# Halo slots of x: transposing transfers in place of GpSimd copies, with a newly searched order

## The chip, the cores and the metric

The kernel runs on one core of a Trainium2 chip. The metric is device time in microseconds, the median of several runs; lower is better. A core has five engines that run at the same time, each through its own list of instructions in order: PE (TensorE, matrix products), DVE (VectorE), ACT (ScalarE), POOL (GpSimd) and SP (which here only issues transfers). DMA engines move data between the chip's main memory and SBUF, the on-chip memory of 128 partitions. PSUM (here called ps) receives what PE computes and is read by DVE and ACT.

## The reference

The input x has 2 sequences of 16000 rows (time steps) of 512 values. The steps are: a depthwise convolution over time with 3 taps, silu, four rounds of residual vector quantization (pick the nearest of 8 code vectors, subtract it), and a second depthwise convolution over the sum of the picked vectors.

```python
xp = jnp.pad(x, ((0,0),(pad,pad),(0,0)))          # pad = 1
for i in range(K):                                # K = 3
    z = z + xp[:, i:i+T, :] * dw_enc[i][None, None, :]
z = _silu(z)
res = z
for s in range(Nq):                               # Nq = 4, C = 8 codes each
    cb = codebooks[s]
    d2 = |res|^2 - 2 res.cb + |cb|^2
    sel = cb[d2.argmin(-1)]
    q = q + sel
    res = res - sel
for i in range(K):
    y = y + qp[:, i:i+T, :] * dw_dec[i][None, None, :]
```

For this study the first loop matters: row t of z needs rows t-1, t and t+1 of x.

## The kernel before

**Tiles.** Each sequence is cut into 9 tiles of G x 128 rows, with G = 6, 8 and seven times 16 in the first sequence and the reverse in the second: 18 tiles, numbered 0 to 17. Neighbouring tiles overlap by four rows, and the outermost rows of a tile at such a joint are not stored, because they lack a true neighbour. Variable `st` describes a tile: `row0` is its first row, G its number of slots.

**Layout of x.** `XT` (two buffers, NX = 2, used by even and odd tiles) holds a tile transposed: the 512 channels lie in 4 groups over 128 partitions; along the free dimension lie G + 2 slots of 128 rows. Row p*G + g of the tile is column p of slot g + 1. So the row before is the same column one slot lower, and the row after one slot higher. The three taps thus read `X[:, i, k:k + G, :]` for k = 0, 1, 2 (line 523). Slots 0 and G + 1 are the halo: slot 0 must hold slot G shifted by one column, and slot G + 1 must hold slot 1 shifted by one column the other way.

**Loading** (`load`, lines 490 to 503). SP issues G transposing transfers for slots 1 to G (line 496). Then POOL fills the halo: the copy at line 502 writes slot 0 from slot G, the copy at line 503 writes slot G + 1 from slot 1. The one column in each halo slot that no row of the tile fills is set to zero (memsets recorded as line 354). A tap reads all G + 2 slots, so it waits for all transfers and both copies; a buffer's next load waits for the taps of two tiles before.

**After the load.** `front` (line 507) runs the taps: six products by a weight for each half of the channels (lines 524 on ACT, 525 on DVE), two additions into ZB (line 367, the line of every DVE tensor_tensor), then exp on ACT (530) and 1 + exp on DVE or ACT. `front2` takes the reciprocal on ACT (542) and multiplies (the gate, 367). `select` (575) scores the first three codebooks on PE (560) and decides on DVE; `windows` (656) transposes the picks into OHW; `resid` (674) subtracts the picked vectors: PE writes the product into ps, and either DVE adds it to ZB (702), or PE adds ZB too (693) and ACT copies the sum back (700); `back` (734) computes the output on PE (751 to 755), ACT moves it from ps to YB (759), and POOL issues the stores (782).

**The order.** No engine's list is written by hand. Every step is handed to a planner (`Plan`, line 17) with an engine, an estimated duration, a key (kind of step, tile, position), and what it reads and writes. `Plan.order` places the steps one by one: the step that could start first, and among equals the one of lowest rank. A rank is made of the tables in `WHEN` (line 248): for each kind of step and for the head, the middle and the tail of the run, an offset in tiles and a slope. `SHARE` says how much DVE's queue must be shorter than ACT's for an eviction of ps to go to DVE; `SLACK` says how much later than DVE ACT may finish an either/or step and still take it; `QUOTA` limits how many pieces of ps may be held for each of the two. The steps are then emitted in that order. The planner also puts filler matmuls (line 802) into PE's gaps. So the durations that the planner is told decide only the order and who does what; what the chip takes is another matter.

Of the kernel before, what the change touches and what calls it, by code (L numbers as in the profile page):

```python
# [12 lines left out]
ACT = mybir.ActivationFunctionType  # L13
# [3 lines left out]
class Plan:  # L17
# [16 lines left out]
    def add(self, engine, cost, key, fn, reads=(), writes=(), take=None, free=None, hold=None, tail=0.0, after=(), dest=None, box=None, mm=0):  # L34
        n = len(self.steps)
        deps = set(after)
        for t in reads:
            if t in self.writer:
                deps.add(self.writer[t])
            self.readers.setdefault(t, []).append(n)  # L40
        for t in writes:
            if t in self.writer:
                deps.add(self.writer[t])
            deps.update(self.readers.get(t, ()))
            self.writer[t] = n
            self.readers[t] = []
        deps.discard(n)
        self.steps.append({"n": n, "e": engine, "c": cost, "k": key, "fn": fn, "deps": sorted(deps), "take": take, "free": free,
                           "hold": hold, "tail": tail, "dest": dest, "box": box, "mm": mm})
        return n  # L50
# [163 lines left out]
def kernel(  # L214
# [8 lines left out]
    nc = tc.nc  # L223
    P = nc.NUM_PARTITIONS
    B, T, D = x.shape
# [16 lines left out]
    PAIR = 1  # L242
    NX, NE, NZ, NOH, NY = 2, 3, 4, 4, 4
    NA = 4
    SHARE = (11.59, 1.54, -2.01)
    SLACK = (0.29, 0.1, -0.82)
    QUOTA = {"ACT": 3, "DVE": 4}
    WHEN = {"setup": ((-0.301, 1.023), (0.403, 0.68), (0.166, 0.636)), "load": ((-2.074, 0.878), (-2.063, 0.738), (-2.063, 0.878)),
            "pad": ((-1.367, 0.11), (-1.736, 0.139), (-2.291, 0.134)), "taps": ((-0.056, 0.643), (-0.338, 0.654), (0.494, 1.172)),
            "exp": ((0.772, 0.385), (0.713, 0.297), (0.924, 0.12)), "plus1": ((1.188, 0.422), (0.353, 0.234), (0.286, 0.554)),  # L250
            "recip": ((0.485, 0.701), (0.412, 0.023), (1.293, 0.525)), "gate": ((-0.006, 0.61), (0.929, 0.495), (1.31, 0.636)),
            "score0": ((-0.15, 0), (1.321, 0.2), (0.126, 0.312)), "decide": ((1.768, 0.427), (0.519, 0.211), (0.108, 0.835)),
            "win0": ((2.318, 0), (2.302, 0), (3.131, 0.025)), "resid": ((1.585, 0.808), (1.683, 0.698), (1.872, 0.836)),
            "score3": ((2.128, 0.792), (2.59, 0.231), (3.148, 1.482)), "decide3": ((1.628, 0.493), (2.782, 0.723), (3.385, 0.635)),
            "win3": ((3.135, 0.158), (3.009, 1.183), (3.633, 0.195)), "back": ((2.837, 0.37), (3.155, 1.136), (4.214, 0.566))}
    assert B == len(SIZES) and T >= GM * P and GM <= 16

    xf = x.flatten_outer_dims()
# [7 lines left out]
    tiles = []  # L266
    for b, sizes in enumerate(SIZES):
        done = 0
        for g in sizes:
            r = g * P  # L270
            t0 = max(0, min(done - 2, T - r))
# [9 lines left out]
    def sb(shape, dt, name):  # L281
        return const.tile(list(shape), dt, name=name)
# [14 lines left out]
    XT = [sb([P, KT, GM + 2, P], BF16, f"XT{b}") for b in range(NX)]  # L297
# [26 lines left out]

    plan = Plan(NA, (3, len(tiles) - 3), SHARE, SLACK, QUOTA, WHEN)
    add = plan.add
# [26 lines left out]
    def pool_memset(t, v, tok, cost, key):  # L353
        add("POOL", cost, key, lambda: nc.gpsimd.memset(t, v), writes=tok)
# [4 lines left out]

    def dve_memset(t, v, tok, cost, key):  # L360
        add("DVE", cost, key, lambda: nc.vector.memset(t, v), writes=tok)

    for b in range(NX):
        pool_memset(XT[b][:, :, 0, 0:2], 0.0, [("XE", b)], 0.3, ("setup", -29, 0))

    def tt(out, a, b, op, cost, key, reads, writes, **kw):
        add("DVE", cost, key, lambda: nc.vector.tensor_tensor(out=out, in0=a, in1=b, op=op), reads, writes, **kw)  # L367
# [122 lines left out]
    def load(st):  # L490
        n, G = st["n"], st["G"]
        X = XT[n % NX]
        src = xf[st["row0"]:st["row0"] + G * P, :].rearrange("(p g) d -> g p d", g=G)

        def one(g):
            nc.sync.dma_start_transpose(out=X[:, :, g + 1, :], in_=src[g])  # L496
        for g in range(G):
            add("SP", 1.56, ("load", n, 0.01 * g), lambda g=g: one(g), [], [("X", n % NX, g + 1)], tail=1.5)
        key = ("pad", n - 20 * (n == 0), 0)
        if n < NX or tiles[n - NX]["G"] != G:  # L500
            pool_memset(X[:, :, G + 1, P - 2:P], 0.0, [("X", n % NX, G + 1)], 0.3, key)
        add("POOL", 1.0, key, lambda: nc.gpsimd.tensor_copy(X[:, :, 0, 1:P], X[:, :, G, 0:P - 1]), [("X", n % NX, G)], [("XE", n % NX)])  # L502
        add("POOL", 1.0, key, lambda: nc.gpsimd.tensor_copy(X[:, :, G + 1, 0:P - 1], X[:, :, 1, 1:P]), [("X", n % NX, 1)], [("X", n % NX, G + 1)])  # L503

    state = {}

# [257 lines left out]
    def store(st, Y, g0, g1):  # L764
# [16 lines left out]
        for p0, p1, lo, hi in split:  # L781
            nc.gpsimd.dma_start(out=view[p0:p1, lo:hi, :], in_=Y[p0:p1, lo - g0:hi - g0, :])  # L782

    load(tiles[0])
    setup()
    for group in GROUPS:
        halves = {}
        for st in group:
            if st["n"]:
                load(st)  # L790
            for h in range(2):
                halves[st["n"], h] = front(st, h)
        for st in group:
            for h in range(2):
                front2(st, h, *halves[st["n"], h])
        for st in group:
            select(st)
            resid(st)
            back(st)
# [40 lines left out]
```

## Time and profile before

| | |
|---|---|
| median of 7 runs | 732.02 us (729.85 to 736.03) |
| profiled run, whole | 733.12 us |
| its span, first to last instruction | 731.3 us |
| mean granted TensorE clock | 0.955 |
| halo copies on POOL, lines 502 and 503 | 18 and 18; busy 23.4 and 33.0 us |
| transposing transfers on SP, line 496 | 252; 1.27 us each in the median to issue, 3.9 us to landing |
| evictions of resid on ACT (700) and on DVE (702) | 287 and 145; busy 246.8 and 150.6 us |
| taps on DVE (525) and on ACT (524) | 205 and 11 |

"Span" is the time between the first and the last instruction; "busy" is the time in which an engine ran at least one instruction. A group is named by its line, its engine and what it writes and reads (`ZB<-ZB,ps` writes ZB and reads ZB and ps). In lists of waits, `A <- B` means that A started when B was done, and the figures are the total in us, the number of times and the longest.

### The profile page before, as it was taken

Reading aid. Unit: us, or ns where it says so; the run is one execution under the profiler, and the core shown is the slowest. Engines: PE = TensorE matmul, PEld = TensorE weight load, DVE = VectorE, ACT = ScalarE, POOL = GpSimd, SP = SyncE. Lnnn points to the kernel's source line nnn. Section 1 sums busy time; section 2 is a strip of 40 time slices with the busy share of each in tenths; the row PEclk is TensorE's granted clock in tenths of the full one; section 3 lists DMA queues with packets and bytes.
Section 4 is the critical chain, followed back from the end, with each engine's and each line's share of the span. In section 5 each row is a group of like instructions: output and inputs, shape, how many; then the busy total and the mean of one; then the engine's idle time right before and its main releaser. Section 6 shows DMA issues by size and latency. Waiting matters only on the chain.

```text
span 731.3 us, 24280 instructions
## 1 busy us (share of the span) xinstructions
PE 577.0 (79%) x10605; PEld 285.4 (39%) x10681; DVE 680.9 (93%) x1251; ACT 666.8 (91%) x590; POOL 133.3 (18%) x199
## 2 busy tenths in 40 slices
PE   5887676796788879798676878778876889899994
PEld 2343232344334434443243343434343444444442
DVE  8989999898999999999999999999999999999892
ACT  6888989889999999999999999999999899998755
POOL 2101022000120331212123302103113110201114
PEclk9999797899989989999999999999999999999998
DMA  5455524625153462818258441716453210303215
GB/s 111 94 95 100 118 53 123 109 46 80 58 125 52 83 122 56 161 54 161 65 125 166 105 73 36 129 46 151 102 90 132 81 38 2 119 5 114 89 45 195
DMA packets 148049, 67.81 MB, mean 93 GB/s; under 512 B 139776, under 2 KB 139808, under 8 KB 147944
## 3 DMA queue, kind: packets, MB, share of 16 engines
q1 hardware_dynamic: 137088, 33.06, 26.6%
q0 software_dynamic: 10640, 32.78, 14.3%
q8 instruction: 83, 1.36, 0.8%
q10 hardware_dynamic: 216, 0.43, 0.2%
q14 instruction: 22, 0.18, 0.1%
HBM read 0.43 MB, written 32.77 MB: 45 GB/s over the span
## 4 chain that ended last, share of the span: by engine, by line
DVE 53%; PE 25%; ACT 10%; issue 7%; DMA 3%; SPq 1%; POOL 0%; DVEq 0%; POOLq 0%; ACTq 0%
DVE ZB L702 12%; PE ps L694 8%; DVE ZB L367 7%; DVE TB L525 7%; PE ps L693 6%; DVE TA L367 6%; PE ps L560 4%; ACT ZB L700 4%; DVE TA L525 3%; ACT YB L759 3%; DVE EX L532 2%; PE ps L802 2%; DMA XT<-in_x_dram 2%; DVE OHW L671 2%; SPq L496 1%
## 5 line engine op out<-in xcount | busy, mean ns | idle before, releaser
L694 PE MATMUL ps<-OHW,CBN 128*128 128x512 bf16 (+1 forms) x768 | 269.3, 388 | 20.1 <-DVE ZB L702 12.8
L700 ACT CAST ZB<-ps 128x1024 bf16<-128x1024 f32 (+2 forms) x287 | 246.8, 953 | 27.4 <-PE ps L694 24.5
L693 PE MATMUL ps<-ZB,IDENT 128*128 128x512 bf16 (+1 forms) x517 | 201.5, 390 | 19.8 <-DVE ZB L702 11.7
L702 DVE TENSOR_TENSOR ZB<-ZB,ps 128x1024 bf16<-128x1024 bf16 (+2 forms) x145 | 150.6, 1054 | 2.2 <-PE ps L694 1.4
L782 POOL DMA_DIRECT2D out_dram<-YB x130 | 74.3, 575 | 352.2 <-ACT YB L759 348.9
L759 ACT CAST YB<-ps 128x1024 bf16<-128x1024 f32 x126 | 123.6, 1041 | 5.1 <-PE ps L751 2.4
L694 PEld LDWEIGHTS <-CBN 128*128 128x128 bf16 x768 | 74.9, 99 | 134.1 <-issue 63.7
L530 ACT ACTIVATE EX<-ZB 128x4096 bf16<-128x4096 bf16 (+2 forms) x36 | 115.5, 3209 | 5.3 <-DVE ZB L367 5.2
L542 ACT ACTIVATE EX<-EX 128x4096 bf16<-128x4096 bf16 (+2 forms) x36 | 114.6, 3194 | 0.2
L560 PEld LDWEIGHTS <-ZB 128*32 128x32 bf16 x8064 | 75.2, 95 | 58.9 <-issue 55.4
L560 PE MATMUL ps<-ZB 128*32 128x64 bf16 x8064 | 88.0, 197 | 12.2 <-issue 5.9
L525 DVE TENSOR_SCALAR TB<-XT,WENC 128x2048 bf16<-128x2048 bf16 (+2 forms) x137 | 92.6, 688 | 0.2
L802 PE MATMUL ps<-MSK,IDENT 128*128 128x512 bf16 x242 | 68.9, 424 | 20.1 <-issue 5.8
L751 PE MATMUL ps<-WDEC,OHW 128*128 128x512 bf16 x219 | 68.0, 381 | 15.2 <-ACT YB L759 3.8
L693 PEld LDWEIGHTS <-IDENT 128*128 128x128 bf16 x517 | 51.7, 100 | 64.8 <-issue 14.6
L367 DVE TENSOR_TENSOR ZB<-ZB,EX 128x4096 bf16<-128x4096 bf16 (+2 forms) x36 | 74.0, 2055 | 1.3 <-ACT EX L542 1.1
L367 DVE TENSOR_TENSOR ZB<-TA,TB 128x4096 bf16<-128x4096 bf16 (+2 forms) x36 | 73.3, 2036 | 0.1
L367 DVE TENSOR_TENSOR TA<-TA,TB 128x4096 bf16<-128x4096 bf16 (+2 forms) x36 | 72.7, 2019 | 0.6 <-ACT TB L524 0.4
L502 POOL COPY XT<-XT 128x508 bf16<-128x508 bf16 x18 | 23.4, 1300 | 165.2 <-DMA XT<-in_x_dram 165.2
L525 DVE TENSOR_SCALAR TA<-XT,WENC 128x2048 bf16<-128x2048 bf16 (+2 forms) x68 | 48.1, 718 | 0.4 <-issue 0.2
L802 PEld LDWEIGHTS <-IDENT 128*128 128x128 bf16 x263 | 26.5, 106 | 51.8 <-issue 30.9
L503 POOL COPY XT<-XT 128x508 bf16<-128x508 bf16 x18 | 33.0, 1836 | 62.0 <-DVE TB L525 51.3
(101 smaller groups left out, 483.7 us busy)
## 6 DMA issues: line engine op xcount, KB each, us to landing
out_dram<-YB POOLq DMA_DIRECT2D x33, 448.0 KB, 4.0
out_dram<-YB POOLq DMA_DIRECT2D x28, 512.0 KB, 4.2
XT<-in_x_dram SPq DMA_TRANSPOSE x252, 3.9
out_dram<-YB POOLq DMA_DIRECT2D x30, 60.0 KB, 4.2
out_dram<-YB POOLq DMA_DIRECT2D x31, 2.0 KB, 2.9
out_dram<-YB POOLq DMA_DIRECT2D x2, 224.0 KB, 2.9
YB<-in_dw_dec_dram ACTq DMA_DIRECT2D x1, 384.0 KB
out_dram<-YB POOLq DMA_DIRECT2D x1, 384.0 KB, 3.6
```

The source lines that it names most:

```text
L367: add("DVE", cost, key, lambda: nc.vector.tensor_tensor(out=out, in0=a, in1=b, op=op), reads, writes, **kw)
L525: lambda dst=dst, src=src, w=w: nc.vector.tensor_scalar(out=dst, in0=src, scalar1=w, scalar2=None, op0=ALU.mult),
L530: add("ACT", act(2 * R), ("exp", n, h), lambda: nc.scalar.activation(v(ex), Z, ACT.Exp, scale=-1.0), zt, [("EX", sl), "ACTTAB"], hold="E")
L542: nc.scalar.add_instruction(mybir.InstActivation(name=nc.get_next_instruction_name(), engine=mybir.EngineType.Activation, func=ACT.Reciprocal,
L560: nc.tensor.matmul(o[HB * q:HB * (q + 1), u * ZW:(u + 1) * ZW].rearrange("p (s c) -> p s c", s=2), lhsT=blk, rhs=both, start=False, stop=( ...
L693: nc.tensor.matmul(o, lhsT=IDENT, rhs=zg[:, k0:k0 + nk, :], start=True, stop=False)
L694: nc.tensor.matmul(o, lhsT=CBN[s, u][:, i * P:(i + 1) * P], rhs=W[:, k0:k0 + nk, PADC:PADC + P], start=not on_act, stop=True)
L700: nc.scalar.copy(zg, v)
L702: nc.vector.tensor_tensor(out=zg, in0=zg, in1=v, op=ALU.add)
L759: add("ACT", act_psum(1024), key, lambda k=k, box=box, Y=Y, k0=k0: nc.scalar.copy(Y[:, 2 * (k - k0):2 * (k - k0) + 2, :].rearrange("p g d ...
L782: nc.gpsimd.dma_start(out=view[p0:p1, lo:hi, :], in_=Y[p0:p1, lo - g0:hi - g0, :])
L802: nc.tensor.matmul(PS[j // 2][:, 512 * (j % 2):512 * (j % 2) + NMK * ZW], lhsT=IDENT, rhs=MSK.rearrange("p u w -> p (u w)"), start=True, s ...
```

## The change

Three things change. First, the halo slots of a tile come from main memory by two more transposing transfers on SP: slot 0 from the rows one before those of slot 1, slot G + 1 from the rows one after those of slot G. Where there is no such row (slot 0 at the start of a sequence, slot G + 1 at its end) and for all of tile 0, POOL's memset and copy stay. The memset of slot 0 at the start of the kernel goes. Second, the planner is told 1.36 us instead of 1.56 for a transfer from tile 2 on. Third, all tables of the order (`SHARE`, `SLACK`, `QUOTA`, `WHEN`) are replaced by others, found by a search in which the durations were varied by seeded noise.

```diff
-    SHARE = (11.59, 1.54, -2.01)
-    SLACK = (0.29, 0.1, -0.82)
-    QUOTA = {"ACT": 3, "DVE": 4}
-    WHEN = {"setup": ((-0.301, 1.023), (0.403, 0.68), (0.166, 0.636)), "load": ((-2.074, 0.878), (-2.063, 0.738), (-2.063, 0.878)),
+    SHARE = (14.72, 0.75, -2.14)
+    SLACK = (-0.24, -0.33, 0.67)
+    QUOTA = {"ACT": 3, "DVE": 3}
+    WHEN = {"setup": ((-0.151, 1.058), (0.208, 0.715), (-0.18, 0.669)), "load": ((-2.06, 0.878), (-1.99, 0.738), (-2.049, 0.878)),
...
-    for b in range(NX):
-        pool_memset(XT[b][:, :, 0, 0:2], 0.0, [("XE", b)], 0.3, ("setup", -29, 0))
-
...
-            add("SP", 1.56, ("load", n, 0.01 * g), lambda g=g: one(g), [], [("X", n % NX, g + 1)], tail=1.5)
+            add("SP", 1.56 if n < 2 else 1.36, ("load", n, 0.01 * g), lambda g=g: one(g), [], [("X", n % NX, g + 1)], tail=1.5)
         key = ("pad", n - 20 * (n == 0), 0)
-        if n < NX or tiles[n - NX]["G"] != G:
-            pool_memset(X[:, :, G + 1, P - 2:P], 0.0, [("X", n % NX, G + 1)], 0.3, key)
-        add("POOL", 1.0, key, lambda: nc.gpsimd.tensor_copy(X[:, :, 0, 1:P], X[:, :, G, 0:P - 1]), [("X", n % NX, G)], [("XE", n % NX)])
-        add("POOL", 1.0, key, lambda: nc.gpsimd.tensor_copy(X[:, :, G + 1, 0:P - 1], X[:, :, 1, 1:P]), [("X", n % NX, 1)], [("X", n % NX, G + 1)])
+        xe, xo = [("XE", n % NX)], [("X", n % NX, G + 1)]
+        r0, t0 = st["row0"], st["row0"] % T
+        if t0 and n:
+            before = xf[r0 - 1:r0 - 1 + G * P, :].rearrange("(p g) d -> g p d", g=G)[0]
+            add("SP", 1.56 if n < 2 else 1.36, ("load", n, 0.01 * G), lambda: nc.sync.dma_start_transpose(out=X[:, :, 0, :], in_=before), [], xe, tail=1.5)
+        else:
+            pool_memset(X[:, :, 0, 0:2], 0.0, xe, 0.3, key)
+            add("POOL", 1.0, key, lambda: nc.gpsimd.tensor_copy(X[:, :, 0, 1:P], X[:, :, G, 0:P - 1]), [("X", n % NX, G)], xe)
+        if t0 + G * P < T and n:
+            behind = xf[r0 + 1:r0 + 1 + G * P, :].rearrange("(p g) d -> g p d", g=G)[G - 1]
+            add("SP", 1.56 if n < 2 else 1.36, ("load", n, 0.01 * G), lambda: nc.sync.dma_start_transpose(out=X[:, :, G + 1, :], in_=behind), [], xo, tail=1.5)
+        else:
+            pool_memset(X[:, :, G + 1, P - 2:P], 0.0, xo, 0.3, key)
+            add("POOL", 1.0, key, lambda: nc.gpsimd.tensor_copy(X[:, :, G + 1, 0:P - 1], X[:, :, 1, 1:P]), [("X", n % NX, 1)], xo)
```

Of the 17 tiles after tile 0, tile 9 keeps the copy for slot 0 (it starts the second sequence), and tiles 8 and 17 keep the one for slot G + 1 (they end a sequence).

## The prediction

> **What bounds the kernel now.** I read the page's busy times first, then a table of busy time by stretch, then who waits for whom, then single instructions. Profiled span 731.3 us, whole profiled run 733.12 us (1.8 us lie around the span). The page's first part and the engine shares of the chain that ended last:
>
> ```profile
> PE 577.0 (79%) x10605; PEld 285.4 (39%) x10681; DVE 680.9 (93%) x1251; ACT 666.8 (91%) x590; POOL 133.3 (18%) x199
> ...
> DVE 53%; PE 25%; ACT 10%; issue 7%; DMA 3%; SPq 1%; POOL 0%; DVEq 0%; POOLq 0%; ACTq 0%
> ```
>
> Two engines are nearly full, and they share the same pool of movable work (evictions of ps, and taps). POOL, which this change relieves, has 18% to do and 0% of the chain. So fewer POOL instructions are worth nothing in themselves; the question is what they do to DVE and ACT. Some stretches, with the columns time, PE, PEld, DVE, ACT, POOL busy (count), clock, DMA share, GB/s:
>
> ```profile
> 51.00:102.00 51.00, 37.19 (x574) 17.36 (x579) 48.92 (x71) 45.84 (x53) 6.25 (x7) 0.90 0.44 90
> ...
> 200.00:300.00 100.00, 81.26 (x1678) 40.90 (x1690) 96.58 (x149) 96.52 (x75) 22.73 (x20) 0.93 0.47 92
> ...
> 660.00:700.00 40.00, 36.72 (x725) 17.66 (x718) 35.51 (x82) 29.18 (x32) 6.89 (x13) 1.00 0.27 94
> 700.00:720.00 20.00, 18.30 (x302) 8.59 (x302) 16.82 (x43) 14.38 (x19) 4.69 (x9) 1.00 0.29 101
> ```
>
> Summing all stretches of that table from 51 to 660 us, DVE is busy 585.6 of 609 us (idle 23.4) and ACT 580.9 (idle 28.1). From 660 to 720 us DVE idles 7.7 us and ACT 16.4. That is the whole room a better order has, beside a start and an end that it can hardly move. What DVE waits for in 51 to 660 us (total, times, longest), top of the list of waits:
>
> ```profile
> DVE PR L615 <- PE ps L560: 3.5, 2, 2.6
> DVE OT L637 <- PE ps L632: 3.1, 3, 1.5
> DVE OHW L671 <- PE ps L560: 2.8, 4, 1.1
> DVE OT L637 <- PE ps L560: 2.4, 5, 0.7
> ```
>
> The whole list sums to 21.1 us, nearly all for PE, and no entry is for a load of x. The loads are early: the clearest case is tile 6, where the copy of its last slot starts once the DMA has landed, at 149.00, and the first tap reads the tile at 162.90, 13.9 us later.
>
> **Where POOL's copies do cost DVE.** Timeline of DVE, two excerpts (start, length, engine, line):
>
> ```profile
> 128.36 2.69 DVE L367 TENSOR_TENSOR ZB<-ZB,EX 128x4096 bf16<-128x4096 bf16 x1
> ...
> 148.40 0.75 DVE L525 TENSOR_SCALAR TA<-XT,WENC 128x2048 bf16<-128x2048 bf16 x1
> 149.06 0.29 DVE L367 TENSOR_TENSOR V<-PR,TR 128x128 bf16<-128x128 bf16 x1
> 149.26 1.10 DVE L525 TENSOR_SCALAR TA<-XT,WENC 128x2048 bf16<-128x2048 bf16 x1
> ```
>
> and POOL alone at that time:
>
> ```profile
> 149.00 0.82 POOL L502 COPY XT<-XT 128x508 bf16<-128x508 bf16 x1 [20.09 <-DMA XT<-in_x_dram]
> ```
>
> The tap that meets the copy takes 1.10 us, its twin 0.75; the gate product at 128.36 takes 2.69, where 2.28 is normal, and a copy of 0.67 us stood on POOL at 128.23. Going through all DVE instructions by shape, 18 are at least 0.15 us over the median of their shape, all 18 overlap a halo copy, and their excess sums to 6.4 us. The reverse is also there: L502 has a mean of 1300 ns and L503 of 1836, against 0.6 us when alone, so the copies are the ones blocked most of the time.
>
> **What the Trainium skill says.** "SBUF — State Buffer", section "Who interferes with whom": GpSimd and VectorE share a port pair under an exclusive lock; tensor_scalar in its fast modes, and tensor_tensor with both inputs in SBUF against a GpSimd instruction that reads SBUF, block or are blocked for the whole instruction. The trace agrees: 0.35 us more for taps, 0.40 for products, in both kinds. The same section says that a DMA never contends with a compute engine; this trace shows no counter-example, since taps and products with loads in flight keep their 0.75 and 2.28 us. "DMA: Bandwidth & Descriptors", section "DMA Transpose (X-bar)", warns of transposes from two streams at once; here old and new ones all stay on SP, so nothing has to be serialized.
>
> **The change part by part.**
>
> 1. Copies removed. 36 halo copies become 5: both of tile 0, slot G+1 of tile 8 (it ends at T), slot 0 of tile 9 (it starts the second batch), slot G+1 of tile 17. Of the 18 lengthened DVE instructions, two (at 11.62 and 12.44 us, 0.4 us each) belong to tile 0 and stay. The others go: 6.4 - 0.8 = 5.6 us of DVE time. DVE passes all of it to the end only if ACT keeps up. ACT is 91% busy; if ACT sets the pace, the saved DVE time must first be turned into evictions moved over from ACT, and half arrives. So 2.8 to 5.6; I take the middle, -4.2. What remains late next is ACT's L700, which waits 24.5 us for PE L694.
>
> 2. Transposes added: 34 - 3 = 31 on SP, each 544 packets in the mean (137088 packets over 252). The rows that price them, from the page's DMA queues and from the view of XT (min/median/max ns):
>
> ```profile
> q1 hardware_dynamic: 137088, 33.06, 26.6%
> ```
>
> ```profile
> L496 SPq DMA_TRANSPOSE XT<-in_x_dram x252: 1188/1265/3595, 0.7 to 589.4; - x126
> ```
>
> 31 more raise q1 from 26.6% to about 29.9% of 16 engines, with total DMA share in the 0.40s: no bound. On SP they are 31 x 1.27 = 39 us at the median, two per tile, so a tile is complete some 3 us later than its last slot was. What hides it: after the last slot landed the copy still had to wait its turn and run (0.6 to 5.3 us), and taps begin over 12 us later. The tight place is the start, where SP issues tiles 0 to 4 with hardly a pause, 62 transposes in 88.4 us, 1.43 us each. Eight more put tile 4 about 11.4 us later, from 88.2 (landing) to 99.6, against its first tap at 102.24: a cover of 2.6 us. Without it, an order that starts tile 4 earlier would stall DVE once; bounds 0 to +4, taken 0.
>
> 3. Waits moved. L503 waits on POOL for the taps of two tiles before (51.3 us in all). Now SP's last transpose of a tile waits for the same readers. Behind it on SP stand only the next tile's loads, which need those readers too. On POOL the parked copies no longer stand ahead of stores; but ACT's wait list shows no wait for a Y buffer to be stored, so that is worth 0. Memsets of XT (8, 0.8 us in all) fall to 5: 0.
>
> 4. The order. All of WHEN, SHARE, SLACK and QUOTA change, so that every engine's queue is rearranged; no row tells what that is worth. SLACK below zero for the head and the middle keeps either/or work on DVE more often: 11 taps run on ACT now (2.0 us each for full tiles, 0.75 on DVE), and a tap returned with an eviction sent the other way saves both about half a microsecond: -2 to 0. QUOTA for DVE from 4 to 3 leaves more of ps to ACT, whose L700 idles for PE. SHARE of the middle from 1.54 to 0.75 pushes evictions to DVE. Bounds: at best half of the named and tail idle of DVE goes (21.1 + 7.7 = 28.8, so -14); at worst it doubles in the middle (+21). An order that is searched with noisy durations should leave producers further ahead, which is what DVE's waits for PE want; I take a third of 28.8 and halve it for PE and ACT, -4.7.
>
> Sum: -4.2 + 0 + 0 - 4.7 = -8.9. Against the profiled run 733.1 - 8.9 = 724.2. That run is 1.1 us above the shown median of 732.02, so the forecast for the median is **723.1 us**.
>
> **The rivals.**
>
> *The stalls go, the time stays.* DVE is freed of 5.6 us, but the new order loses as much in waits for PE, or ACT is the true pace. For: DVE and ACT differ by 14 us of busy time only, and ACT waits 24.5 us for L694. Against: 53% of the chain is DVE. Time 732.0 - 5.6 + 5 = about 731.
>
> *Slower: consumers too close behind PE.* The new order puts the small decision steps of one tile, or their evictions, before PE has the product; DVE then stands, as at 131.24 to 133.88 us now, where it waits 2.64 us for L560. Place: the middle, among L610, L615, L637, L671, L718. Price: the 21.1 us grow by half to a doubling, 10 to 21 us, less the 5.6 saved. It decides from 27 us of such waits on. For: a quota of 3 lets PE run less far ahead of DVE, and the list is fragile (30 waits of about 0.7 us). Against: waits are already only 3.5% of the middle. Time 732.0 + 15 - 5.6 = about 741.
>
> *The change doesn't do what it says* (halo transposes so late that DVE waits for x): first sight would be a DVE or ACT wait for XT. Only the start is open to it, +4 at most; it is folded into the others.
>
> **How the numbers follow.** About 0.3% (2.2 us) is what a measurement of this kernel can tell from no change. Forecast case: 0.58, own range 712 to 729. Stalls go and time stays: 0.14, 729 to 734. Slower: 0.28, 735 to 748. Nearly all of the middle case counts as no change, with a little of it going to each side: faster 0.58, same 0.13, slower 0.29. The range leaves out the lowest 0.05 of the first case and the upper end of the third: 713 to 742.
>
> **What would show it.** Right: no DVE instruction of the taps or products over its shape's median outside the five copies left; DVE's busy time down about 5 us for the same split; DVE's waits for PE in the middle under 20 us; 283 transposes on SP; no wait of DVE or ACT for XT past 20 us. Step 2 is wrong if DVE waits for XT before 110 us. Step 4 is wrong if the middle's waits exceed 27 us, if the tail's idle grows, or if the sum of DVE and ACT busy time (1347.7 us now) rises because more either/or work sits on the dearer engine. Then the time would be above 735.

## The result, and the profile after

The changed kernel takes **740.43 us** in the median (12 runs, 738.67 to 742.94), the kernel before 731.8 us in the runs beside it: ratio 1.0118, 95% interval 1.0094 to 1.0141. It is slower by some 8.6 us, where 723.1 had been forecast. The figure lies inside the stated range, on the other side of zero.

The first lines of the page of the changed kernel, busy times and the engines' shares of the chain that ended last:

```profile
PE 587.2 (79%) x10655; PEld 291.9 (39%) x10732; DVE 674.1 (91%) x1257; ACT 656.4 (89%) x584; POOL 87.4 (12%) x165
...
DVE 53%; PE 19%; ACT 13%; issue 8%; DMA 4%; SPq 3%; POOL 1%; DVEq 0%; another core or an unknown queue 0%; POOLq 0%; ACTq 0%
```

Both busy engines have less to do: DVE 674.1 instead of 680.9 us, ACT 656.4 instead of 666.8. The span grew all the same, from 731.3 to 740.5 us. So nothing that an instruction of these two costs explains the loss; on both it is all idle time, 66.4 instead of 50.4 us on DVE and 84.1 instead of 64.5 on ACT. Only PE is busier, by 10.2 us, and that is filler matmuls, which compute nothing that is used. The two groups, first in the kernel before (line 802), then in the changed one (line 810):

```profile
L802 PE MATMUL ps<-MSK,IDENT 128*128 128x512 bf16 x242 | 68.9, 424 | 20.1 <-issue 5.8
```

```profile
L810 PE MATMUL ps<-MSK,IDENT 128*128 128x512 bf16 x290 | 78.9, 419 | 22.3 <-DVE S L603 6.8
```

Was it the loads? The view of XT in the changed kernel (ns are min/median/max):

```profile
L494 SPq DMA_TRANSPOSE XT<-in_x_dram x252: 1189/1265/3391, 0.7 to 594.1; - x126
L533 DVE TENSOR_SCALAR TB<-XT,WENC x140: 412/748/764, 14.2 to 658.9; 128x2048 bf16<-128x2048 bf16 x110, 128x1024 bf16<-128x1024 bf16 x16, 128x768 bf16<-128x768 bf16 x14
L533 DVE TENSOR_SCALAR TA<-XT,WENC x71: 410/747/897, 13.5 to 653.1; 128x2048 bf16<-128x2048 bf16 x55, 128x768 bf16<-128x768 bf16 x8, 128x1024 bf16<-128x1024 bf16 x8
L502 SPq DMA_TRANSPOSE XT<-in_x_dram x16: 1264/1264/2054, 19.1 to 595.4; - x16
L508 SPq DMA_TRANSPOSE XT<-in_x_dram x15: 1264/1264/1913, 20.4 to 554.3; - x15
```

The 31 new transposes (L502, L508) cost 1.26 us each in the median to issue, as the old ones. The longest tap into TB now takes 764 ns; it was 1098. One tap into TA takes 897 ns, at 279.01 us, beside one of the five copies that are left (275.37 to 279.36 us). Only two DVE instructions, both beside such a copy, are still at least 0.15 us over the median of their shape, 0.8 us in all; there were 18 with 6.4 us. Among all waits of DVE none is for x, and ACT's only one is in the setup. So the halo part did what it should. The stretches, with the columns of the table of before (time, PE, PEld, DVE, ACT, POOL busy, clock, DMA share, GB/s), first the changed kernel, then the one before from 500 us on:

```profile
51.00:102.00 51.00, 38.63 (x530) 18.82 (x536) 45.90 (x74) 38.58 (x40) 1.75 (x3) 0.94 0.54 105
...
500.00:600.00 100.00, 78.29 (x1596) 39.49 (x1605) 90.27 (x167) 90.94 (x72) 10.26 (x20) 0.90 0.50 97
600.00:660.00 60.00, 51.23 (x1048) 26.46 (x1040) 54.65 (x129) 56.02 (x49) 5.51 (x11) 0.97 0.16 55
...
700.00:720.00 20.00, 17.83 (x277) 8.33 (x278) 18.20 (x48) 12.73 (x17) 3.24 (x7) 1.00 0.23 83
```

```profile
500.00:600.00 100.00, 79.28 (x1817) 40.76 (x1829) 95.72 (x160) 95.85 (x75) 21.64 (x30) 0.97 0.44 102
600.00:660.00 60.00, 55.82 (x1045) 27.91 (x1050) 58.56 (x137) 58.33 (x55) 5.97 (x11) 1.00 0.14 46
```

Three stretches stand out. From 51 to 102 us DVE lost 3.0 us of busy time and ACT 7.3. From 500 to 600 us DVE fell from 95.72 to 90.27 and ACT from 95.85 to 90.94. From 600 to 660 us DVE lost another 3.9 and ACT 2.3. What DVE waited for in 51 to 660 us, and what PE's fillers waited for:

```profile
DVE ZB L710 <- PE ps L702: 6.9, 6, 4.0
DVE PR L623 <- PE ps L568: 5.6, 4, 2.2
...
DVE OT L645 <- PE ps L640: 4.0, 1, 4.0
```

```profile
PE ps L810 <- DVE S L603: 6.8, 3, 3.6
PE ps L810 <- DVE RC L618: 5.6, 2, 3.4
```

Two waits of DVE are 4.0 us long, against 2.6 for the longest before. Both stand behind a batch of fillers. The first, in PE's and then in DVE's timeline of the changed kernel (idle time before, and what ended it, in brackets). L640 transposes the picks of one codebook (OHA), L645 copies the transpose out of ps (OT), L650 computes from it a correction, and L618 reads that from ps for the next pick (RC):

```profile
68.28 0.26 PE L650 MATMUL ps<-BD,OT 64*128 64x64 bf16 x3
71.98 5.73 PE L810 MATMUL ps<-MSK,IDENT 128*128 128x512 bf16 x17 [3.44 <-DVE RC L618]
77.64 0.24 PE L640 MATMUL ps<-IDENT,OHA 128*64 128x128 bf16 x1
```

```profile
69.37 2.30 DVE L365 TENSOR_TENSOR ZB<-TA,TB 128x4096 bf16<-128x4096 bf16 x1
...
71.70 0.22 DVE L618 TENSOR_TENSOR RC<-ps,S 128x64 f32<-128x64 f32 x1
...
73.15 0.22 DVE L365 TENSOR_TENSOR OHA<-KEY,M 128x64 bf16<-128x64 f32 x1
...
77.92 0.22 DVE L645 COPY OT<-ps 64x128 bf16<-64x128 bf16 x1 [4.04 <-PE ps L640]
```

PE's list says: 17 fillers, then the transpose L640. The fillers write into a bank of ps that DVE has still to read (RC, L618), so PE stands 3.44 us. When the bank is free at last, PE first works through 5.73 us of fillers. The pick OHA that L640 needs had been ready since 73.37 us; DVE waits for L640 until 77.92. RC itself came late because DVE's list has other work ahead of it: L650, whose result it reads, was done at 68.54 us, but DVE, busy all the time, ran an addition of 2.30 us first. The second, PE and then DVE:

```profile
521.83 0.50 PE L650 MATMUL ps<-BD,OT 128*128 128x128 bf16 x3 [0.68 <-DVE OT L645]
524.50 3.15 PE L810 MATMUL ps<-MSK,IDENT 128*128 128x512 bf16 x7 [2.17 <-DVE RC L618]
527.44 0.63 PE L701 MATMUL ps<-ZB,IDENT 128*128 128x512 bf16 x1
```

```profile
521.89 2.28 DVE L365 TENSOR_TENSOR ZB<-TA,TB 128x4096 bf16<-128x4096 bf16 x1
...
524.17 0.28 DVE L618 TENSOR_TENSOR RC<-ps,S 128x128 f32<-128x128 f32 x1
...
531.77 1.22 DVE L710 TENSOR_TENSOR ZB<-ZB,ps 128x1024 bf16<-128x1024 bf16 x1 [3.98 <-PE ps L702]
```

The same addition stands ahead of RC. Here the real products L701 and L702 stand behind the fillers, ACT waits 6.3 us for them and DVE 4.0. The longest wait of a filler is elsewhere, and ends at 99.78 us:

```profile
99.78 0.58 PE L810 MATMUL ps<-MSK,IDENT 128*128 128x512 bf16 x1 [3.61 <-DVE S L603]
```

There ACT stands 4.61 us (until 103.26), but DVE doesn't.

### The profile page after: what moved, and what is told of

Same layout as the page of the kernel before. It is cut to its first block, busy times and chain, and to the rows that moved or that the text cites. A ratio compares the mean times of both kernels' runs of the same rounds, so it can differ in the third digit from the quotient of the medians.

```text
span 740.5 us, 24334 instructions
## 1 busy us (share of the span) xinstructions
PE 587.2 (79%) x10655; PEld 291.9 (39%) x10732; DVE 674.1 (91%) x1257; ACT 656.4 (89%) x584; POOL 87.4 (12%) x165
## 3 DMA queue, kind: packets, MB, share of 16 engines
q1 hardware_dynamic: 153952, 37.13, 31.2%
## 4 chain that ended last, share of the span: by engine, by line
DVE 53%; PE 19%; ACT 13%; issue 8%; DMA 4%; SPq 3%; POOL 1%; DVEq 0%; another core or an unknown queue 0%; POOLq 0%; ACTq 0%
DVE ZB L710 12%; DVE ZB L365 9%; DVE TB L533 7%; DVE TA L365 5%; PE ps L702 5%; ACT ZB L708 4%; DVE TA L533 4%; PE ps L701 4%; PE ps L568 3%; ACT EX L550 3%; DMA XT<-in_x_dram 3%; ACT EX L538 3%; PE ps L810 3%; SPq L494 3%; DVE EX L540 2%
## 5 line engine op out<-in xcount | busy, mean ns | idle before, releaser
L702 PE MATMUL ps<-OHW,CBN 128*128 128x512 bf16 (+1 forms) x768 | 265.7, 384 | 17.5 <-DVE ZB L710 6.1
L701 PE MATMUL ps<-ZB,IDENT 128*128 128x512 bf16 (+1 forms) x524 | 203.0, 387 | 22.4 <-DVE ZB L710 11.7
L710 DVE TENSOR_TENSOR ZB<-ZB,ps 128x1024 bf16<-128x1024 bf16 (+2 forms) x142 | 145.7, 1046 | 8.0 <-PE ps L702 7.4
L790 POOL DMA_DIRECT2D out_dram<-YB x130 | 76.6, 594 | 602.2 <-ACT YB L767 537.6
L702 PEld LDWEIGHTS <-CBN 128*128 128x128 bf16 x768 | 75.3, 99 | 130.5 <-issue 62.4
L568 PE MATMUL ps<-ZB 128*32 128x64 bf16 x8064 | 90.8, 197 | 17.3 <-issue 8.4
L568 PEld LDWEIGHTS <-ZB 128*32 128x32 bf16 x8064 | 76.9, 95 | 56.3 <-issue 52.5
L810 PE MATMUL ps<-MSK,IDENT 128*128 128x512 bf16 x290 | 78.9, 419 | 22.3 <-DVE S L603 6.8
L701 PEld LDWEIGHTS <-IDENT 128*128 128x128 bf16 x524 | 52.2, 100 | 64.7 <-issue 12.8
L810 PEld LDWEIGHTS <-IDENT 128*128 128x128 bf16 x307 | 30.9, 105 | 57.9 <-issue 31.3
L540 DVE TENSOR_SCALAR EX<-EX 128x4096 bf16<-128x4096 bf16 (+2 forms) x36 | 39.2, 1089 | 1.8 <-ACT EX L538 1.8
L759 PEld LDWEIGHTS <-OHW 128*128 128x128 bf16 x252 | 23.1, 99 | 44.2 <-issue 21.8
```

The source lines that it names most:

```text
L568: nc.tensor.matmul(o[HB * q:HB * (q + 1), u * ZW:(u + 1) * ZW].rearrange("p (s c) -> p s c", s=2), lhsT=blk, rhs=both, start=False, stop=( ...
L701: nc.tensor.matmul(o, lhsT=IDENT, rhs=zg[:, k0:k0 + nk, :], start=True, stop=False)
L702: nc.tensor.matmul(o, lhsT=CBN[s, u][:, i * P:(i + 1) * P], rhs=W[:, k0:k0 + nk, PADC:PADC + P], start=not on_act, stop=True)
L710: nc.vector.tensor_tensor(out=zg, in0=zg, in1=v, op=ALU.add)
L759: nc.tensor.matmul(o, lhsT=W[:, k, PADC:PADC + P], rhs=WDEC[u], start=True, stop=not wrap)
L810: nc.tensor.matmul(PS[j // 2][:, 512 * (j % 2):512 * (j % 2) + NMK * ZW], lhsT=IDENT, rhs=MSK.rearrange("p u w -> p (u w)"), start=True, s ...
```

## The experiments

**1. The two parts apart.** The first run keeps the lists of PE, DVE and ACT exactly as in the kernel before and swaps only the halo; the second keeps those of the changed kernel and puts the copies on POOL back.

```diff
 # e1: the planner still sees the two POOL steps; they emit nothing where a transfer fills the slot
+        def last(g):
+            one(g)
+            if g == G - 1 and low:
+                nc.sync.dma_start_transpose(out=X[:, :, 0, :], in_=...)   # rows one before
+            if g == G - 1 and high:
+                nc.sync.dma_start_transpose(out=X[:, :, G + 1, :], in_=...)   # rows one after
 # e2: the planner still sees the two SP steps; they emit nothing, the copies are emitted when the tile has landed
+            j = add("SP", ..., lambda: None, [], xe, tail=1.5)
+            later[j] = copy0
```

> PE, DVE and ACT run exactly the lists of the kernel before; only the halo differs: 31 of 36 copies on POOL are replaced by two transposes at the end of each tile's loads on SP. Theory 'order' (the new order is what costs, the halo part gains): ratio to before 0.991 to 0.997, 725 to 730 us, no lengthened taps or products. Rival 'transposes' (31 more transfers delay x, or the work around them): ratio 1.008 or more, 738 us or above. A third reading, that the stalls are not worth anything because ACT paces DVE: ratio 0.998 to 1.002.

> The mirror image: PE, DVE and ACT run exactly the lists of the changed kernel, and the halo is copied on POOL soon after a tile has landed, as before. Theory 'order': slower than the changed kernel by the stalls that come back, ratio to before 1.013 to 1.022, 742 to 748 us. Rival 'transposes': the loss goes, ratio 0.998 to 1.003. Third reading (stalls worth nothing): 1.010 to 1.013, as the changed kernel.

Measured: 730.18 us, ratio 0.998 (0.9962 to 0.9998), and 745.34 us, ratio 1.0195 (1.0152 to 1.0239). The rival "transposes" is out: in both orders the transfers are the better halo. The loss belongs to the order, some 10 us of it (1.0118 against 0.998). But the gain of the halo in the old order is 1.5 us (by the interval 0.1 to 2.8), not the 5.6 of DVE's stalls; it misses what was expected of "order", and 0.998 is the edge of the third reading. The page of that run shows where the freed time went:

```profile
PE 579.6 (79%) x10605; PEld 286.9 (39%) x10681; DVE 674.3 (92%) x1251; ACT 666.9 (91%) x590; POOL 86.6 (12%) x165
...
DVE 44%; PE 27%; ACT 18%; issue 10%; DMA 1%; DVEq 0%; POOL 0%; ACTq 0%; POOLq 0%
```

DVE is freed of 6.6 us of busy time; its share of the chain falls from 53% to 44%, PE and ACT take it over, and DVE's waits in 51 to 660 us rise from 20.8 to 24.2 us. In the new order the same swap is worth about 5 us (745.34 to 740.43; six runs of e2, 742.0 to 752.4). Why it is worth more there was not taken apart; in e2 DVE has 58% of the chain.

**2. Are the new tables bad?** The tables were exchanged between the two kernels, each with its own halo; the planner then makes new orders.

> Kernel before with nothing changed but SHARE, SLACK, QUOTA and WHEN, taken from the changed kernel; the planner makes an order of its own from them, not the changed kernel's. Theory 'order' in the sense that these tables are worse wherever they are used: 738 us or more. If only the one order that came out for the changed kernel is bad, this one may lie anywhere from 728 to 745. Rival 'transposes': 730 to 734.

> Changed kernel with SHARE, SLACK, QUOTA and WHEN of the kernel before; again the planner makes an order of its own. Theory 'order', tables worse everywhere: 725 to 732 us. If an order is only as good as the one plan for which its tables were searched, it loses too: 735 to 745 us. Rival 'transposes': 738 us or above as well, so that this run decides only together with the one that keeps the old lists exactly.

Measured (e3, then e4): 740.53 us (ratio 1.0121, 1.0089 to 1.0153) and 756.0 us (1.0323, 1.0286 to 1.036). The second says that the old tables are not good by themselves: with the steps of the new halo they give the slowest kernel so far, above both ranges that "order" allowed for it. So one more thing was varied, a single estimate that the planner is told.

```diff
-            add("SP", 1.56, ("load", n, 0.01 * g), ...)          # j1, kernel before
+            add("SP", 1.55, ("load", n, 0.01 * g), ...)
-            add("SP", 1.56 if n < 2 else 1.36, ("load", ...)      # j2, changed kernel, at all three places
+            add("SP", 1.56 if n < 2 else 1.37, ("load", ...)
```

> Kernel before with one estimate changed: the planner is told 1.55 instead of 1.56 us for a transfer of x. Same work, same tables, same halo copies. Theory 'single plan' (a kernel is as fast as the one plan its tables were picked for, and any change of the steps or of an estimate gives another plan at random): 745 us or more. Theory 'tables' (the old tables are good, the new ones bad): 729 to 735 us.

> Changed kernel with one estimate changed: the planner is told 1.37 instead of 1.36 us for a transfer from tile 2 on. Theory 'single plan': another plan at random, 745 to 760 us, as the kernel before with its estimate changed (756.8). If tables that were searched under noise are robust against such a change, as the search intends: 736 to 745 us.

Measured: 756.79 us (ratio 1.0319, 1.0274 to 1.0365) and 751.88 us (1.0265, 1.0226 to 1.0304). What is computed is the same; 0.01 us in one estimate costs 25 and 11 us. These runs show neither set of tables to be the better one: the old tables gave 732, 756 and 757 us for three plans, the new ones 740, 741 and 752. Whether tables searched under noise are better on average can't be read from three plans each.

These plans differ in who does the work, too. In j1 DVE has 155 of the evictions of resid instead of 145 and is busy 692.8 us instead of 680.9; in j2 157 instead of 142, and 685.5 instead of 674.1 us. In e3 DVE is busy 691.1 us and in e4 691.6, against 680.9 and 674.1 in the kernels with the same halo. In e3, e4 and j2 the extra busy time is as much as the whole loss against that kernel, and DVE idles no longer than there (47.6, 65.6 and 60.9 us, against 50.4, 66.4 and 66.4); in j1 it is half. So a plan can lose in another way than the changed kernel does, by the split of the work between DVE and ACT. No run separates the two ways in these four plans.

**3. What in the new plan costs the time.** The fillers compute nothing that is used, so single batches can be left out while everything else in every list stays.

```diff
-            if s["fill"]:
+            if s["fill"] and not 72.0 < s["t"] < 73.0 and not 497.5 < s["t"] < 498.5:    # f1; g1 only the second
 # f2, f3: if s["fill"] and s["t"] < 66.0     (s["t"]: the planner's time)
```

> Changed kernel with two batches of filler matmuls left out (17 at 72 us, 7 at 524 us), all other instructions and orders the same; the fillers compute nothing that is used. These two are the batches where PE first waited for DVE to free a bank of ps and DVE then stood for 4.7 and 3.9 us. If the fillers cause these holes: 733 to 737 us, ratio to before 1.002 to 1.007. If the waits come from the order of the real work and the fillers only sit in the hole: 739 to 742, as the changed kernel.

> Changed kernel with only the batch of 7 filler matmuls at 524 us left out (they compute nothing that is used). In the run with both batches out, tile 12 was already 3.0 us ahead and tile 13 8.1 us, so if the two add up: 734 to 737 us, the rest of the 7.8 us being the batch at 72 us. If one hole absorbs the other: 732 to 733 or 739 to 741.

> Changed kernel without any filler matmul after about 70 us (they compute nothing that is used). If the changed kernel loses by its larger number of fillers (290 in its trace against 242), it gains here: below 738 us. If the fillers pay by keeping PE's clock up: above 743 us. If they matter little: 738 to 743.

> Kernel before without any filler matmul after about 70 us, the control for the run above. If fillers explain the difference of the two kernels, the two runs without them meet, within 3 us. If not, about 8 us stay between them: this one 730 to 735 us when fillers matter little.

| fillers | new order | old order |
|---|---|---|
| all | 740.43 us, 1.0118 | 731.8 us, 1 |
| without the batch at 524 us | 736.36 us, 1.004 (1.0022 to 1.0057) | |
| without those at 72 and 524 us | 732.63 us, 1.0007 (0.9989 to 1.0026) | |
| none after about 70 us | 734.31 us, 1.0033 (1.0016 to 1.005) | 739.37 us, 1.0091 (1.0057 to 1.0125) |

Two batches, 24 matmuls of some 10,600, account for 7.8 of the 8.6 us, more than expected (733 to 737 us). The later one alone is worth 4.1 us by the times and 5.7 by the ratios, which allow for the kernel before taking 732.0 us beside one of these runs and 732.8 beside the other; the earlier one is left with 3.7 or 2.4. No run leaves out the earlier one alone, so how the loss divides is known only roughly. With both out, the stretch from 500 to 600 us is as full as in the kernel before, while 600 to 660 us stays at 55.04 us of DVE:

```profile
500.00:600.00 100.00, 78.57 (x1689) 40.66 (x1684) 96.11 (x177) 96.47 (x75) 10.59 (x21) 0.97 0.47 101
```

PE's timeline with both left out, at the place of the second hole:

```profile
516.98 0.34 PE L650 MATMUL ps<-BD,OT 128*128 128x128 bf16 x3 [0.77 <-DVE OT L645]
517.15 0.38 PE L701 MATMUL ps<-ZB,IDENT 128*128 128x512 bf16 x1
517.37 0.38 PE L702 MATMUL ps<-OHW,CBN 128*128 128x512 bf16 x1
...
519.65 0.58 PE L701 MATMUL ps<-ZB,IDENT 128*128 128x512 bf16 x1 [1.47 <-DVE RC L618]
```

After L650 the real products start at once, 0.17 us later; with the fillers it took 5.6 us (521.83 to 527.44). The wait for RC comes four products later and is 1.47 us long. The last row of the table says that fillers as such are no mistake: in the old order their absence costs 7.4 us (four runs), at a mean granted clock of 0.921 instead of 0.955; neither expectation for that run had it. In the new order it gains 6.1, because the two bad batches go with the rest: against the run without those two it is 1.7 us slower, and the intervals overlap.

**4. More of the same.** Nine batches of the new order (g2) that began with a wait for DVE or stood beside idle time were left out, and eight such batches of the old order with the halo by DMA (g3).

> Changed kernel without the nine batches of fillers that began with a wait for DVE or stood beside idle time of DVE or ACT in its trace (at 72, 100, 132, 134, 264, 268, 379, 524 and 639 us), the others kept; they compute nothing that is used. Theory 'fillers that wait for a bank': faster than with two left out, 726 to 732 us, ratio to before 0.992 to 1.0. If only the two large ones mattered: 731 to 734. If the smaller ones were needed for PE's clock: 733 or more.

> Old order with the halo by DMA (the run e1) without the eight batches of fillers that in the trace of before began with a wait for DVE of 1.4 us or more, or stood beside idle time of both engines (at 128, 130, 146, 236, 379, 428, 541 and 566 us); they compute nothing that is used. Theory 'fillers that wait for a bank': 725 to 729 us, ratio to before 0.990 to 0.996. If this order has no such hole: 729 to 732, as e1.

Measured: 731.08 us, ratio 0.9981 (0.996 to 1.0003), and 730.47 us, ratio 0.9965 (0.9946 to 0.9984). Each interval overlaps that of the run it builds on (f1 and e1), so beyond the two large batches nothing more is shown to have been gained. Among the nine is the batch at 99.78 us, with the longest wait of a filler and 4.6 us of ACT standing behind it. So neither the wait of a filler nor an engine standing behind it is enough to tell that a batch costs time at the end. The last run has the lowest ratio of the study, 0.35% faster than the kernel before.

## Why the prediction was wrong

**Step 4, the order, failed.** The term -4.7 rested on the thought that an order searched with noisy durations would leave producers further ahead of consumers. Measured in its place: about +10 us (1.0118 against the 0.998 of the same halo in the old order), 7.8 of them from two batches of fillers. The step priced SHARE, SLACK and QUOTA, and the taps moved as it said (DVE has 211 of them instead of 205; the sum of DVE and ACT busy time fell from 1347.7 to 1330.5 us, 6.6 of it by the copies). It left out the third thing that an order places, the fillers, and so put their cost at nothing. The page of before had shown them, 242 matmuls at L802 with 20.1 us of idle PE before them. The planner puts fillers where its own times leave PE idle, into the bank that its own times set free first (lines 157 to 160). By that code a batch is over at least 0.6 us before the step behind it. In the plan this step comes at 72.5 us for the first batch and at 498.0 for the second (the planner's times, from the edit of g2); on the chip the fillers began at 71.98 and 524.50 us, because DVE read the bank only then, and the steps behind them at 77.64 and 527.44. In PE's fixed list the filler held up whatever stood behind it. So chip and plan drift apart, by 5 us at the first batch and 29 at the second. That RC stands behind an addition of 2.3 us in DVE's list is in the trace; why the plan expected it earlier was not traced. Some 2 us of the 10 (1.0007 with the two batches out, 0.998 in the old order) stay without a place; the two intervals overlap.

**Step 1, the copies, was right in kind and too large in size.** The stalls are gone (DVE 6.6 us less busy with the same lists), but -4.2 turned out as -1.5 us in the old order and about -5 in the new. The stated lower end, half of 5.6, is the far end of the interval of that run (0.1 to 2.8 us). The rival in which the stalls go and the time stays gave 731 us and is nearly what the halo alone did in the old order: PE and ACT took over the chain. Two small slips change nothing: the list of DVE's waits adds up to 20.8 us, not 21.1, and a third of 28.8, halved, is 4.8.

**Steps 2 and 3 held.** Neither DVE nor ACT waited for x past the setup, and the loads' queue q1 rose to 31.2%, against 29.9% estimated:

```profile
q1 hardware_dynamic: 153952, 37.13, 31.2%
```

The section "Who interferes with whom" of the page "SBUF — State Buffer" in the Trainium skill is borne out by the swap in e2: with the copies back on POOL, 16 DVE instructions are again at least 0.15 us over the median of their shape; 15 of them overlap a copy, and their excess is 5.2 us in all.

**The slower rival had the time and the symptom, not the cause.** It gave 741 us and put the turning point at 27 us of DVE waits in the middle; the changed kernel has 36.9, and with two batches of fillers out 27.2, at the time of before. (DVE's busy time and these waits together are 701.7 us in the kernel before, 711.0 in the changed one and 701.0 without the two batches.) But it expected decision steps placed too close behind PE. What stood in the way was work that nobody needs. The chances had put 0.58 on faster for an order of which no row told the worth; the runs with 0.01 us changed show that the spread among plans, 732 to 757 us, is wider than the whole sum of -8.9. That the loss came so close to the slower rival's 741 is luck: its price stood for another cause.

## What to carry to other kernels

Where a change comes with a newly planned order, price the two apart: keep the old lists and swap only the part, before saying what the part is worth. Filler work stands in an engine's fixed list like any other: look for fillers that begin with a wait for another engine and have the fullest engine standing behind them, leave those out first, and measure, since of the nine batches left out here, all beside waits or idle time, only two are shown to have cost time. In a replanned order, look at the busy time of the fullest engine as well as at its holes. And a planned order that comes out by 25 us differently for 0.01 us in one estimate should be picked by running several plans on the chip; its tables did not carry over to other steps here (756.0 us).

## What had not been expected of the hardware

Fillers are worth 7.4 us in the old order (739.37 without, 732.0 beside it), and with them goes the granted clock of PE, 0.921 without and 0.955 with: about 1% here, though PE is only 79% busy and two other engines are the fuller ones. That it is the clock that pays was not separated; in the new order the clock is 0.927 without fillers and 0.961 without the two batches in the profiled runs, for 1.7 us that are not clear of noise.

In the second hole PE also ran at the slower pace: its matmuls start 0.43 us apart (527.44, 527.87, 528.30) up to 529.15 us and 0.22 apart from 529.56 on, and the 7 fillers took 3.15 us at that pace. Without the two batches the products behind the wait of 1.47 us also start 0.43 us apart, from 520.03 us up to 522.59. So in these two places the first products that the other engines wait for were the slow ones.
